# A fused attention and expert kernel: shorter steps for distance and mask tables, paired loads of plain operands, identity products at the start

## The chip, the cores and the metric

The kernel runs on one core of a Trainium2 chip. The metric is the device time of one execution in microseconds (us). The kernel before was run three times: median 1122.09 us, 1121.79 to 1123.15. Line numbers (L892) are those of the kernel before, as its profile gives them.

## The reference

Local attention with a few global columns, then two chains of matrix products. For 4 batches and 8 heads of 64 over 768 positions:

```
scores = q @ k.T / 8
keep   = (column < n_global) | (0 <= row - column < n_local)
dist   = n_local where global and not local, else |row - column|
scores = where(keep, scores - slope[head] * dist, -1e9)
x      = softmax(scores) @ v                  # 3072 tokens of 512
x      = (((x @ w1) * (x @ w2)) @ w3) @ w_out
h      = x @ w_in;   out = (h * cos(h)) @ w_out2
```

`n_global` (8) and `n_local` (96) arrive as 64-bit integers, and the weights as 64-bit floating-point words, which the kernel turns into 32-bit ones itself (the "decoding").

## The kernel before

**Units and chunks.** Attention is cut into 96 units: 128 rows of one pair of heads. A unit's scores are 128 rows by 232 columns for each of its two heads: 128 of its own block, 96 before it and 8 global ones; the first block of a batch has the 128 alone. While `w3 @ w_out` is folded into one matrix in 16 chunks (the loop over `chunks`, c = 0 to 15; a chunk is four 512-wide products, two instructions each at L892), the first 14 units are worked on beside it, unit n = c - 1 in chunk c. A block loop over the remaining units and the products of the experts follows, and then the last part.

**The order in a chunk** is written out by hand and is the order of each engine's queue: the scaled copies of the tables for two heads (`bias_heads`, ScalarE, L514 and L515, in chunks 0 to 3), scores of unit n (TensorE, L575), the load of the plain operands of unit n + 2, values of unit n - 3 (L672), the minimum with the bias (VectorE, L606), decode steps, the exponentials (ScalarE, L617), two of the four products (L892), transposes of unit n - 2 (L645, L647), their copy to SBUF (ScalarE, L655 or L660), the scaling of unit n - 1 by its reciprocal sums (VectorE L627 and L630, ScalarE L636), more decode steps, the other two products.

**Decoding** (`decoder`, a generator called one step at a time). For each weight of 512 KB: a load on SyncE's queue (L325), two passes on ScalarE (L338, L339), then three steps on VectorE: shift (L343), sign (L347), sum (L355). Six buffers hold raw weights, so a load waits for the sum of the sixth weight before it, and whatever stands behind it in SyncE's queue waits too. A chunk needs two decoded weights.

**Before the chunks.** A ScalarE queue loads `v0` (the first values and the two integers) and unit 0's plain operands, and SyncE the first weights. `biases` builds two tables, `dist` (128 by 232) and `d0` (128 by 128), of distances with a very large number where nothing is kept: two casts, then `scalars` (five small steps that turn the integers into floats), four steps ahead of 21 decode steps, and ten more steps, one behind each decode step from the eighth on. The identity for transposes is made on GpSimd. TensorE's first instructions are the scores of unit 0.

**Plain operands.** The first 22 units (`PLAIN`) take queries and keys as they are in 32 bits; a row of 64 partitions holds them, and the input holds them twice, in the lower and the upper 64 partitions. `a_load_plain` puts one unit into the lower half of a tile `hh`, of which there are two, so the load of unit n + 2 waits for the scores of unit n.

Of the kernel before, what the change touches and what calls it, by code (L numbers as in the profile page):

```python
# [8 lines left out]
F32 = mybir.dt.float32  # L9
F32R = mybir.dt.float32r  # L10
I32 = mybir.dt.int32
# [12 lines left out]
LOC, GLB = 96, 8  # L24
# [245 lines left out]
def fused(ctx, tc, a_qk, a_v, a_v0, w3p, wo1p, w1p, w2p, winp, wo2p, out):  # L270
# [164 lines left out]
                )  # L435


    def scalars():
        raw = v0[:, 256:].bitcast(I32).rearrange("p (a b) -> p a b", b=2)
        lo = misc.tile([128, 2], F32, name="nlo")  # L440
        hi = misc.tile([128, 2], F32, name="nhi")
        ng = misc.tile([128, 2], F32, name="nneg")
        nv = misc.tile([128, 2], F32, name="nval")
        nc.vector.tensor_copy(out=lo, in_=raw[:, :, 0])
        nc.vector.tensor_copy(out=hi, in_=raw[:, :, 1])
        nc.vector.tensor_scalar(ng, lo, 0.0, None, ALU.is_lt)
        nc.vector.tensor_tensor(out=hi, in0=hi, in1=ng, op=ALU.add)
        nc.vector.scalar_tensor_tensor(
            out=nv, in0=hi, scalar=4294967296.0, in1=lo, op0=ALU.mult, op1=ALU.add
        )  # L450
        yield nv

    def biases(tp):

        rel = tp.tile([128, 128 + LOC], I32, name="rel")
        col = tp.tile([128, 128], I32, name="col")
        nc.gpsimd.iota(rel[:, 0:128], pattern=[[-1, 128]], base=0, channel_multiplier=1)
        nc.gpsimd.iota(rel[:, 128:], pattern=[[-1, LOC]], base=LOC, channel_multiplier=1)
        nc.gpsimd.iota(col, pattern=[[1, 128]], base=0, channel_multiplier=0)
        dist = tp.tile([128, WIN], F32, name="dist")  # L460
        colf = tp.tile([128, 128], F32, name="colf")
        keep = tp.tile([128, WIN], F32, name="keep")
        lt = rel.bitcast(F32)
        gl = tp.tile([128, 128], F32, name="gl")
        tmp = col.bitcast(F32)
        d0 = tp.tile([128, 128], F32, name="d0")
        nr = 128 + LOC
        nc.vector.tensor_copy(out=dist[:, :nr], in_=rel)
        nc.vector.tensor_copy(out=colf, in_=col)
        yield  # L470
        nv = next(scalars())
        nl, ng = nv[:, 0:1], nv[:, 1:2]
        yield nv
        nc.vector.tensor_scalar(lt[:, :nr], dist[:, :nr], nl, None, ALU.is_lt)
        yield
        nc.vector.scalar_tensor_tensor(
            out=keep[:, :nr], in0=dist[:, :nr], scalar=0.0, in1=lt[:, :nr],
            op0=ALU.is_ge, op1=ALU.mult,
        )
        yield  # L480
        nc.vector.tensor_scalar(gl, colf, ng, None, ALU.is_lt)
        yield
        nc.vector.tensor_copy(out=keep[:, nr:], in_=gl[:, :GLB])
        yield

        nc.vector.tensor_tensor(out=tmp, in0=gl, in1=keep[:, :128], op=ALU.mult)
        yield
        nc.vector.tensor_tensor(out=gl, in0=gl, in1=tmp, op=ALU.subtract)
        yield
        nc.vector.scalar_tensor_tensor(  # L490
            out=tmp, in0=dist[:, :128], scalar=nl, in1=gl, op0=ALU.subtract, op1=ALU.mult
        )
        yield
        nc.vector.tensor_tensor(out=d0, in0=dist[:, :128], in1=tmp, op=ALU.subtract)
        yield
        nc.vector.tensor_tensor(out=tmp, in0=gl, in1=keep[:, :128], op=ALU.add)
        yield

        nc.vector.tensor_scalar(tmp, tmp, -1.0, -FAR, ALU.add, ALU.mult)
        yield  # L500
        nc.vector.tensor_scalar(keep, keep, -1.0, -FAR, ALU.add, ALU.mult)
        yield
        nc.vector.tensor_scalar(dist[:, nr:], colf[:, :GLB], 0.0, nl, ALU.mult, ALU.add)
        yield
        nc.vector.tensor_tensor(out=d0, in0=d0, in1=tmp, op=ALU.add)
        yield
        nc.vector.tensor_tensor(out=dist, in0=dist, in1=keep, op=ALU.add)
        yield d0, dist

    def bias_heads(d0, dist, heads):  # L510

        for h in heads:
            s = -8.0 * 2.0 ** (-8.0 * (h + 1) / H)
            nc.scalar.activation(bias0[:, h, :], d0, ACTF.Copy, scale=s)  # L514
            nc.scalar.activation(bias1[:, h, :], dist, ACTF.Copy, scale=s)  # L515


    def where(n):
        j, r = divmod(n, UPB)
        p, i = divmod(r, TPB)  # L520
        return j, p, i, (TPB * j + i) % (S // 128)
# [8 lines left out]
        nc.sync.dma_start(out=t, in_=a_qk[n])  # L530
        qk_raw[n] = t

    def a_load_plain(n, queue=None):

        if not 0 <= n < PLAIN:
            return
        t = plain[n] = attn.tile([128, QK_W], F32R, tag="hh", name="hh")[0:64].bitcast(F32)
        (queue or nc.sync).dma_start(out=t, in_=a_qk[n, 0:64])

    def a_load_v(n):  # L540
        if not 1 <= n < NU:
# [26 lines left out]
    def a_scores(n):  # L568
        if not 0 <= n < NU:
            return  # L570
        s_ps[n] = p_s.tile([128, 2, WIN], F32, tag="s", name="s_ps")
        if n in plain:
            t, w = plain.pop(n), WIN if where(n)[3] else 128
            for e in range(2):
                nc.tensor.matmul(  # L575
                    s_ps[n][:, e, :w], lhsT=t[:, e * 128:(e + 1) * 128],
                    rhs=t[:, 256 + e * WIN:256 + e * WIN + w], start=True, stop=True,
                )
            return
        t, l = hh.pop(n), kl.pop(n)  # L580
        for e in range(2):
            q = t[:, e * 128:(e + 1) * 128]
            nc.tensor.matmul(  # L583
                s_ps[n][:, e, :], lhsT=q, rhs=t[:, 256 + e * WIN:256 + (e + 1) * WIN],
                start=True, stop=False,
            )
            nc.tensor.matmul(  # L587
                s_ps[n][:, e, :], lhsT=q, rhs=l[:, e * WIN:(e + 1) * WIN],
                start=False, stop=True,
            )  # L590
# [186 lines left out]
    with tc.manual_schedule():  # L777
# [85 lines left out]
        v0 = early.tile([128, 260], F32, name="v0")  # L863
        nc.scalar.dma_start(out=v0, in_=a_v0)
        v_raw[0] = v0[:, :256].rearrange("p (a b) -> p a b", a=2)
        a_load_plain(0, nc.scalar)
        a_scores(0)
        nc.vector.memset(pt_ps, 0.0)
        steps_b = biases(tp)
        next(steps_b)  # L870
        make_identity(nc, ident)
        nv = next(steps_b)
        for _ in range(4):
            next(steps_b)
        dists = None
        for i in range(21):
            decode(1)
            if i == 0:
                a_load_plain(1)
            elif i == 12:  # L880
                a_load_v(1)
            if i > 6:
                dists = dists or next(steps_b)
        W_ps = {}
        for c, (h, k) in enumerate(chunks):
# [18 lines left out]

            a_load(own + 3)
            a_load_v(n - 1 if n > 2 else -1)
            if c < 4:
                bias_heads(*dists, range(2 * c, 2 * c + 2))
            elif c == 4:
                tp.release()  # L910
            if n > 0:
                a_scores(own)
            if n >= 0:
                a_load_plain(own + 2)
            a_values(n - 3)
            a_max(own)
# [509 lines left out]
```

## Time and profile before

| | |
|---|---|
| median of three runs | 1122.09 us |
| profiled execution | 1120.99 us, span 1119.0 us |
| TensorE (PE) | 1100.0 us busy, 98% |
| VectorE (DVE) | 776.6 us, 69% |
| ScalarE (ACT) | 680.4 us, 61% |
| GpSimd (POOL) | 78.8 us, 7% |
| mean granted clock of TensorE | 0.998 of 2.4 GHz |

The span runs from the first to the last instruction. A share is an average over stages: TensorE is full nearly everywhere, the other engines are full in some stretches only. The chain of waits is followed back from the last instruction, so it names at each time the work that the end hung on. `[1.83 <-DVE wo L355]` behind an instruction means that its engine was idle for 1.83 us and that VectorE's L355 ended the idle time. PEld is TensorE's weight load, a q behind an engine its queue. The granted clock of a stretch is given as a share (0.50 is 1.2 GHz).

### The profile page before, as it was taken

Reading aid. Unit: us, or ns where it says so; the run is one execution under the profiler, and the core shown is the slowest. Engines: PE = TensorE matmul, PEld = TensorE weight load, DVE = VectorE, ACT = ScalarE, POOL = GpSimd, SP = SyncE. Lnnn points to the kernel's source line nnn. Section 1 sums busy time; section 2 is a strip of 40 time slices with the busy share of each in tenths; the row PEclk is TensorE's granted clock in tenths of the full one; section 3 lists DMA queues with packets and bytes.
Section 4 is the critical chain, followed back from the end, with each engine's and each line's share of the span. In section 5 each row is a group of like instructions: output and inputs, shape, how many; then the busy total and the mean of one; then the engine's idle time right before and its main releaser. Section 6 shows DMA issues by size and latency. Waiting matters only on the chain.

```text
span 1119.0 us, 17357 instructions
## 1 busy us (share of the span) xinstructions
PE 1100.0 (98%) x6034; PEld 953.0 (85%) x6034; DVE 776.6 (69%) x1661; ACT 680.4 (61%) x1370; POOL 78.8 (7%) x161
## 2 busy tenths in 40 slices
PE   5999999999999999999999999999999999999997
PEld 2456999999999999999999888888888888888886
DVE  8888666767576675778726588884777883877841
ACT  7998766657566676677725466662555561655531
POOL 0000001111111111112200001000000000000000
PEclk9999999999999999999999999999999999999999
DMA  8865545555555556477575545659474458564261
GB/s 305 267 212 177 171 154 187 161 171 165 171 160 180 161 156 194 137 253 237 176 245 189 181 148 214 214 195 377 136 305 179 130 202 346 182 251 170 86 233 60
DMA packets 86480, 219.22 MB, mean 196 GB/s; under 512 B 9328, under 2 KB 25968, under 8 KB 86384
## 3 DMA queue, kind: packets, MB, share of 16 engines
q1 hardware_dynamic: 86016, 217.57, 57.2%
q8 instruction: 50, 0.82, 0.3%
q10 hardware_dynamic: 368, 0.45, 0.1%
q14 instruction: 46, 0.38, 0.1%
HBM read 178.14 MB, written 39.85 MB: 195 GB/s over the span
## 4 chain that ended last, share of the span: by engine, by line
PE 96%; DVE 2%; DMA 1%; issue 0%; ACT 0%; SPq 0%; DVEq 0%
PE mm L432 36%; PE o_ps L432 23%; PE h_ps L432 20%; PE mm L892 4%; PE x_ps L672 4%; PE pt_ps L645 2%; PE s_ps L575 2%; PE pt_ps L647 2%; PE s_ps L587 1%; PE s_ps L583 1%; DMA hh<-in_a_qk 1%; DVE r L1121 0%; DMA v<-in_a_v 0%; DVE w L347 0%; DVE w L355 0%
## 5 line engine op out<-in xcount | busy, mean ns | idle before, releaser
L432 PE MATMUL o_ps<-o,g 128*128 128x512 f32 x960 | 223.3, 389 | 0.0
L432 PEld LDWEIGHTS o_ps<-o,g 128*128 128x128 f32 x960 | 180.0, 188 | 37.6
L432 PE MATMUL mm<-ab,W 128*128 128x384 f32 x768 | 147.0, 342 | 0.0
L432 PE MATMUL mm<-xT,wA 128*128 128x384 f32 x768 | 146.4, 341 | 0.0
L432 PE MATMUL mm<-xT,wB 128*128 128x384 f32 x768 | 146.2, 341 | 0.0
L432 PE MATMUL h_ps<-T,piece 128*128 128x512 f32 x576 | 142.7, 391 | 0.1
L432 PEld LDWEIGHTS mm<-ab,W 128*128 128x128 f32 x768 | 131.5, 188 | 2.7 <-issue 2.4
L432 PEld LDWEIGHTS mm<-xT,wA 128*128 128x128 f32 x768 | 131.1, 188 | 2.1 <-issue 1.8
L432 PEld LDWEIGHTS mm<-xT,wB 128*128 128x128 f32 x768 | 130.9, 188 | 2.1 <-issue 2.1
L432 PEld LDWEIGHTS h_ps<-T,piece 128*128 128x128 f32 x576 | 108.0, 188 | 23.9 <-DVE gr L1235 0.5
L551 ACT CAST hh<-qk 128x720 fp32r<-128x720 f32 x74 | 58.8, 795 | 111.4 <-PE s_ps L587 104.1
L432 PE MATMUL h_ps<-B,piece 128*128 128x512 f32 x432 | 106.5, 390 | 0.0
L638 POOL TENSOR_SCALAR e<-e,st 128x232 f32<-128x232 f32 x148 | 71.8, 496 | 484.3 <-DVE st L630 414.7
L432 PEld LDWEIGHTS h_ps<-B,piece 128*128 128x128 f32 x432 | 81.0, 188 | 17.7 <-DVE vv L1235 0.4
L617 ACT ACTIVATE e<-e,top 128x232 f32<-128x232 f32 (+1 forms) x192 | 89.1, 467 | 1.9 <-DVE top L606 1.8
L606 DVE CUSTOM_DVE_ANT_0 e<-s_ps,bias 128x232 f32<-128x232 f32 (+1 forms) x192 | 65.4, 378 | 31.6 <-PE s_ps L587 27.5
L1127 ACT ACTIVATE r<-r 128x1024 f32<-128x1024 f32 x48 | 51.0, 1062 | 32.4 <-DVE r L1121 32.0
L715 DVE TENSOR_TENSOR a_sb<-mm,a_sb 128x384 f32<-128x384 f32 x64 | 35.6, 556 | 44.4 <-PE mm L432 41.6
L892 PE MATMUL mm<-wo,w 128*128 128x512 f32 x128 | 64.6, 635 | 1.8 <-DVE wo L355 1.8
L1121 DVE SCALAR_TENSOR_TENSOR r<-kt,r 128x1024 f32<-128x1024 int32 x48 | 58.8, 1224 | 1.5
L1140 ACT CAST g<-gr 128x512 fp32r<-128x512 f32 x48 | 29.0, 621 | 42.6 <-PE o_ps L432 42.5
L1145 DVE TENSOR_TENSOR g<-gr,g 128x512 fp32r<-128x512 f32 x48 | 31.7, 687 | 32.4 <-ACT g L1140 32.4
(136 smaller groups left out, 1689.0 us busy)
## 6 DMA issues: line engine op xcount, KB each, us to landing
piece<-a_s SPq DMA_DIRECT2D x84, 512.0 KB, 5.6
o<-o2s SPq DMA_DIRECT2D x80, 512.0 KB, 5.9
qk<-in_a_qk SPq DMA_DIRECT2D x74, 360.0 KB, 3.2
a_s<-ap SPq DMA_DIRECT2D x56, 256.0 KB, 2.4
v<-in_a_v SPq DMA_DIRECT2D x95, 128.0 KB, 3.1
raw<-in_w3p SPq DMA_DIRECT2D x16, 512.0 KB, 5.4
raw<-in_winp SPq DMA_DIRECT2D x16, 512.0 KB, 4.4
raw<-in_wo2p SPq DMA_DIRECT2D x16, 512.0 KB, 4.7
```

What stands on the lines that cost most here:

```text
L432: nc.tensor.matmul(ps, lhsT=l, rhs=r, start=first and i + e == 0, stop=last and i == n - 1 and e == 2, skip_group_check=more,)
L551: nc.scalar.copy(out=hh[n], in_=qk_raw[n])
L606: nc.vector.tensor_tensor_reduce(out=es[n][:, e, :w], in0=sp[:, e, :w], in1=bias[:, 2 * p + e, :], scale=-0.125, scalar=3.0e38, op0=ALU.ad ...
L617: nc.scalar.activation(es[n][:, e, :w], es[n][:, e, :w], ACTF.Exp, bias=top[:, n, e:e + 1], scale=-1.0, accum_out=sts[n][:, 0, e:e + 1],)
L638: nc.gpsimd.tensor_scalar(x, x, st[:, 1, e:e + 1], 1.0, ALU.mult, ALU.mult)
L672: nc.tensor.matmul(x[e * 64:(e + 1) * 64, i * 128:(i + 1) * 128], lhsT=vt[:kk, c, e * 64:(e + 1) * 64], rhs=pt[:kk, e, c, :], start=c == 0 ...
L715: nc.vector.tensor_tensor(out=t, in0=mm_ps.pop("b"), in1=t, op=ALU.mult)
L892: nc.tensor.matmul(W_ps[m], lhsT=wt["w3", c][:, m * 128:(m + 1) * 128], rhs=wt["wo1", k], start=k == 0, stop=k == M1 - 1,)
L1121: nc.vector.scalar_tensor_tensor(out=self.r, in0=self.kt, scalar=-c, in1=self.h if c == C1 else self.r, op0=ALU.mult, op1=ALU.add,)
L1127: nc.scalar.activation(self.r, self.r, ACTF.Sin, scale=0.5)
L1140: nc.scalar.copy(out=t[:, 0, :], in_=src[:, m, :])
L1145: nc.vector.tensor_tensor(out=t[:, 1, :], in0=src[:, m, :], in1=t[:, 0, :].bitcast(F32), op=ALU.subtract,)
```

## The change

`biases` makes the tables in fewer steps. One select on GpSimd puts 2^80 where a column is ahead of its row. Three steps turn the integers into floats. After that come five steps, all between decode steps: distances of `n_local` and more get a multiple of 2^40 added, columns that aren't global 2^120, and `d0` is the smaller of both. `bias_heads` for heads 2 to 7 moves to chunks 3, 6 and 9. A plain tile holds two units, the even one in the lower, the odd one in the upper 64 partitions; one load of 360 KB fetches both (the odd unit from the lower copy in the input and the even one from the upper copy ahead of it). Units 0 and 1 are still loaded apart; the tile of units 2 and 3 is asked for behind the eleventh decode step. Twenty products of the identity with itself, 128 wide, go to TensorE ahead of the scores of unit 0.

```diff
--- before.py
+++ after.py
@@ -435,21 +435,6 @@
                 )
 
 
-    def scalars():
-        raw = v0[:, 256:].bitcast(I32).rearrange("p (a b) -> p a b", b=2)
-        lo = misc.tile([128, 2], F32, name="nlo")
-        hi = misc.tile([128, 2], F32, name="nhi")
-        ng = misc.tile([128, 2], F32, name="nneg")
-        nv = misc.tile([128, 2], F32, name="nval")
-        nc.vector.tensor_copy(out=lo, in_=raw[:, :, 0])
-        nc.vector.tensor_copy(out=hi, in_=raw[:, :, 1])
-        nc.vector.tensor_scalar(ng, lo, 0.0, None, ALU.is_lt)
-        nc.vector.tensor_tensor(out=hi, in0=hi, in1=ng, op=ALU.add)
-        nc.vector.scalar_tensor_tensor(
-            out=nv, in0=hi, scalar=4294967296.0, in1=lo, op0=ALU.mult, op1=ALU.add
-        )
-        yield nv
-
     def biases(tp):
 
         rel = tp.tile([128, 128 + LOC], I32, name="rel")
@@ -459,53 +444,47 @@
         nc.gpsimd.iota(col, pattern=[[1, 128]], base=0, channel_multiplier=0)
         dist = tp.tile([128, WIN], F32, name="dist")
         colf = tp.tile([128, 128], F32, name="colf")
-        keep = tp.tile([128, WIN], F32, name="keep")
-        lt = rel.bitcast(F32)
-        gl = tp.tile([128, 128], F32, name="gl")
-        tmp = col.bitcast(F32)
-        d0 = tp.tile([128, 128], F32, name="d0")
+        past = rel.bitcast(F32)
+        words = misc.tile([128, 2, 2], F32, name="words")
+        nv = misc.tile([128, 2], F32, name="nval")
+        nl, ng = nv[:, 0:1], nv[:, 1:2]
         nr = 128 + LOC
         nc.vector.tensor_copy(out=dist[:, :nr], in_=rel)
         nc.vector.tensor_copy(out=colf, in_=col)
+        nc.gpsimd.affine_select(
+            out=dist[:, :128], in_=dist[:, :128], compare_op=ALU.is_ge, fill=2.0 ** 80,
+            base=0, pattern=[[-1, 128]], channel_multiplier=1,
+        )
         yield
-        nv = next(scalars())
-        nl, ng = nv[:, 0:1], nv[:, 1:2]
+        lo, hi = words[:, :, 0], words[:, :, 1]
+        nc.vector.tensor_copy(
+            out=words.rearrange("p a b -> p (a b)"), in_=v0[:, 256:].bitcast(I32)
+        )
+        nc.vector.scalar_tensor_tensor(
+            out=hi, in0=lo, scalar=0.0, in1=hi, op0=ALU.is_lt, op1=ALU.add
+        )
+        nc.vector.scalar_tensor_tensor(
+            out=nv, in0=hi, scalar=4294967296.0, in1=lo, op0=ALU.mult, op1=ALU.add
+        )
         yield nv
-        nc.vector.tensor_scalar(lt[:, :nr], dist[:, :nr], nl, None, ALU.is_lt)
+        nc.vector.scalar_tensor_tensor(
+            out=past, in0=dist[:, :nr], scalar=nl, in1=dist[:, :nr],
+            op0=ALU.is_ge, op1=ALU.mult,
+        )
         yield
         nc.vector.scalar_tensor_tensor(
-            out=keep[:, :nr], in0=dist[:, :nr], scalar=0.0, in1=lt[:, :nr],
-            op0=ALU.is_ge, op1=ALU.mult,
+            out=dist[:, :nr], in0=past, scalar=2.0 ** 40, in1=dist[:, :nr],
+            op0=ALU.mult, op1=ALU.add,
         )
         yield
-        nc.vector.tensor_scalar(gl, colf, ng, None, ALU.is_lt)
+        nc.vector.tensor_scalar(colf, colf, ng, FAR, ALU.is_ge, ALU.mult)
         yield
-        nc.vector.tensor_copy(out=keep[:, nr:], in_=gl[:, :GLB])
-        yield
-
-        nc.vector.tensor_tensor(out=tmp, in0=gl, in1=keep[:, :128], op=ALU.mult)
-        yield
-        nc.vector.tensor_tensor(out=gl, in0=gl, in1=tmp, op=ALU.subtract)
+        nc.vector.tensor_scalar(dist[:, nr:], colf[:, :GLB], nl, None, ALU.add)
         yield
         nc.vector.scalar_tensor_tensor(
-            out=tmp, in0=dist[:, :128], scalar=nl, in1=gl, op0=ALU.subtract, op1=ALU.mult
-        )
-        yield
-        nc.vector.tensor_tensor(out=d0, in0=dist[:, :128], in1=tmp, op=ALU.subtract)
-        yield
-        nc.vector.tensor_tensor(out=tmp, in0=gl, in1=keep[:, :128], op=ALU.add)
-        yield
-
-        nc.vector.tensor_scalar(tmp, tmp, -1.0, -FAR, ALU.add, ALU.mult)
-        yield
-        nc.vector.tensor_scalar(keep, keep, -1.0, -FAR, ALU.add, ALU.mult)
-        yield
-        nc.vector.tensor_scalar(dist[:, nr:], colf[:, :GLB], 0.0, nl, ALU.mult, ALU.add)
-        yield
-        nc.vector.tensor_tensor(out=d0, in0=d0, in1=tmp, op=ALU.add)
-        yield
-        nc.vector.tensor_tensor(out=dist, in0=dist, in1=keep, op=ALU.add)
-        yield d0, dist
+            out=colf, in0=colf, scalar=nl, in1=dist[:, :128], op0=ALU.add, op1=ALU.min
+        )
+        yield colf, dist
 
     def bias_heads(d0, dist, heads):
 
@@ -530,12 +509,17 @@
         nc.sync.dma_start(out=t, in_=a_qk[n])
         qk_raw[n] = t
 
-    def a_load_plain(n, queue=None):
-
-        if not 0 <= n < PLAIN:
+    def a_load_plain(n, both=True, queue=None):
+
+        if n % 2 and both or not 0 <= n < PLAIN:
             return
-        t = plain[n] = attn.tile([128, QK_W], F32R, tag="hh", name="hh")[0:64].bitcast(F32)
-        (queue or nc.sync).dma_start(out=t, in_=a_qk[n, 0:64])
+        if n % 2 == 0:
+            plain[n // 2] = attn.tile([128, QK_W], F32R, tag="hh", name="hh").bitcast(F32)
+        lo, hi = n % 2 * 64, 128 if both else n % 2 * 64 + 64
+        (queue or nc.sync).dma_start(
+            out=plain[n // 2][lo:hi],
+            in_=a_qk.rearrange("n p c -> (n p) c")[n * 128 + 64:][0:hi - lo],
+        )
 
     def a_load_v(n):
         if not 1 <= n < NU:
@@ -569,8 +553,9 @@
         if not 0 <= n < NU:
             return
         s_ps[n] = p_s.tile([128, 2, WIN], F32, tag="s", name="s_ps")
-        if n in plain:
-            t, w = plain.pop(n), WIN if where(n)[3] else 128
+        if n < PLAIN:
+            t = plain[n // 2][n % 2 * 64:n % 2 * 64 + 64]
+            w = WIN if where(n)[3] else 128
             for e in range(2):
                 nc.tensor.matmul(
                     s_ps[n][:, e, :w], lhsT=t[:, e * 128:(e + 1) * 128],
@@ -863,20 +848,23 @@
         v0 = early.tile([128, 260], F32, name="v0")
         nc.scalar.dma_start(out=v0, in_=a_v0)
         v_raw[0] = v0[:, :256].rearrange("p (a b) -> p a b", a=2)
-        a_load_plain(0, nc.scalar)
-        a_scores(0)
+        a_load_plain(0, False, nc.scalar)
         nc.vector.memset(pt_ps, 0.0)
         steps_b = biases(tp)
         next(steps_b)
         make_identity(nc, ident)
+        warm = p_s.tile([128, 2, WIN], F32, tag="s", name="warm")
+        for _ in range(20):
+            nc.tensor.matmul(warm[:, 0, 0:128], lhsT=ident, rhs=ident, start=True, stop=True)
+        a_scores(0)
         nv = next(steps_b)
-        for _ in range(4):
-            next(steps_b)
         dists = None
         for i in range(21):
             decode(1)
             if i == 0:
-                a_load_plain(1)
+                a_load_plain(1, False)
+            elif i == 10:
+                a_load_plain(2)
             elif i == 12:
                 a_load_v(1)
             if i > 6:
@@ -904,13 +892,13 @@
 
             a_load(own + 3)
             a_load_v(n - 1 if n > 2 else -1)
-            if c < 4:
-                bias_heads(*dists, range(2 * c, 2 * c + 2))
-            elif c == 4:
+            if c % 3 == 0 and c < 12:
+                bias_heads(*dists, range(2 * c // 3, 2 * c // 3 + 2))
+            elif c == 10:
                 tp.release()
             if n > 0:
                 a_scores(own)
-            if n >= 0:
+            if n > 0:
                 a_load_plain(own + 2)
             a_values(n - 3)
             a_max(own)
```

## Rows read from the trace of the kernel before

**Rows 1.** The chain of waits, 0 to 40 us: start us, us, what.
```profile
5.01 0.17 DVE nlo L444
...
5.80 0.35 DVE rel L474
...
6.88 0.43 DVE w L343
...
11.82 0.20 DVE col L486
...
17.36 0.20 DVE d L505
...
21.40 5.63 DMA hh<-in_a_qk
27.16 1.02 PE s_ps L575 x4
...
37.08 1.72 PE mm L892 x4
```

**Rows 2.** Busy time by stretch: us, each engine's busy us, PEclk, DMA share, GB/s.
```profile
20.00:25.00 5.00, 4.68 (x13) 2.11 (x12) 5.00 (x15) 4.36 (x13) 0.00 (x0) 1.00 0.86 277
...
60.00:70.00 10.00, 10.00 (x42) 5.05 (x41) 9.99 (x30) 10.00 (x27) 0.00 (x0) 1.00 0.76 256
```

**Rows 3.** TensorE in order of time: start us, us, instruction [idle before <-releaser].
```profile
7.76 1.22 PE L575 MATMUL s_ps<-hh 64*128 64x128 f32 x4 [7.76 <-DMA hh<-in_a_qk]
...
10.81 9.26 PE L892 MATMUL mm<-wo,w 128*128 128x512 f32 x16 [1.83 <-DVE wo L355]
...
20.98 3.70 PE L892 MATMUL mm<-wo,w 128*128 128x512 f32 x8
...
31.05 0.23 PEld L645 LDWEIGHTS pt_ps<-ident,e 128*128 128x128 f32 x1 [0.15 <-ACT e L636]
```

**Rows 4.** GpSimd, ScalarE and VectorE in order of time, columns as in rows 3.
```profile
1.64 0.33 POOL masks.py:199 TENSOR_SCALAR_AFFINE_SELECT ident<-ident 128x128 f32<-128x128 f32 x1
...
10.31 0.67 ACT L338 ACTIVATE wo<-raw 128x512 f32<-128x512 f32 x1 [0.62 <-DMA raw<-in_wo1p]
...
26.85 0.40 DVE L606 CUSTOM_DVE_ANT_0 e<-s_ps,bias 128x232 f32<-128x232 f32 x1
...
27.18 0.29 ACT L514 ACTIVATE bias<-d 128x128 f32<-128x128 f32 x1
...
28.16 0.47 ACT L617 ACTIVATE e<-e,top 128x232 f32<-128x232 f32 x1
...
30.21 0.68 ACT L636 ACTIVATE e<-e,st 128x128 f32<-128x128 f32 x2
```

**Rows 5.** Busy time in single microseconds, columns as in rows 2.
```profile
11.00:12.00 1.00, 1.00 (x2) 0.48 (x3) 0.96 (x4) 0.55 (x1) 0.00 (x0) 1.00 1.03 410
...
28.00:29.00 1.00, 1.00 (x3) 0.49 (x3) 1.00 (x4) 1.00 (x4) 0.00 (x0) 0.89 1.05 254
29.00:30.00 1.00, 1.00 (x2) 0.33 (x1) 1.00 (x4) 1.00 (x4) 0.00 (x0) 0.50 1.03 273
...
32.00:33.00 1.00, 1.00 (x3) 0.38 (x2) 1.00 (x5) 1.00 (x6) 0.00 (x0) 0.90 1.06 304
```

**Rows 6.** ScalarE's copies L655, L660 and TensorE's L672, columns as in rows 3.
```profile
60.60 0.56 ACT L655 COPY pt<-pt_ps 128x512 f32<-128x512 f32 x1
...
61.48 0.66 PE L672 MATMUL x_ps<-pt,v 128*64 128x128 f32 x8
...
65.77 0.34 ACT L660 COPY pt<-pt_ps 128x256 f32<-128x256 f32 x1
...
66.56 0.44 PE L672 MATMUL x_ps<-pt,v 128*64 128x128 f32 x4
```

**Rows 7.** ScalarE's waits from 40 to 70 us (total, times, longest us).
```profile
ACT e L617 <- DVE top L606: 1.2, 1, 1.2
...
ACT pt L660 <- PE pt_ps L645: 0.2, 1, 0.2
```

## The prediction

> **What bounds the kernel now.** I read the engine totals first: TensorE is busy for 98% of the span, so what the change wins must come from the few stretches in which TensorE isn't fed at full rate. All its parts lie in the first 110 us. So I followed the chain of waits from 0 to 40 us [rows 1]. It runs over VectorE (weight decoding and the tables) from 5 us, then over the load of the third unit's plain operands, `hh`, issued at 21.40 and 5.63 us under way, and then over TensorE. From 37 us on four instructions of L892 take 1.72 us, 0.43 each [rows 1]; the first sixteen took 9.26 us in place of 6.9 [rows 3].
>
> Read like this, TensorE has several things to win: the half-rate start (2.4 us), an earlier first product, the `hh` wait. But another view decides. VectorE is busy in 5.00 of the 5 us from 20 to 25 [rows 2], and the first transpose, that of unit 0, waited at 31.05 for ScalarE's scaling `e` (L636) [rows 3]. TensorE and the chain over VectorE and ScalarE arrive there together, so what TensorE alone wins before 31 us becomes a wait at that transpose. The question is how much earlier this chain gets there.
>
> **The change part by part.**
>
> *Table steps.* VectorE starts at 5.01, when `v0` has landed; five small steps take it to 5.80 [rows 1], so three take 0.5 to 0.6: saved 0.2. The four steps ahead of the decoding, from 5.80 to 6.88 [rows 1], go behind it: 1.08 earlier. Of the ten steps between decode steps (first and last 0.20 each [rows 1], ten make 2.0) five remain. Two are 224 wide, like L474 (0.35 where it waits for its forerunner [rows 1]); between decode steps I price them at 0.3, the other three at 0.15 to 0.25: 1.2, saved 0.8. One wait is new: the fourth weight's first ScalarE pass runs from 10.31 to 10.98 [rows 4], and VectorE now asks for it some 0.2 before that. So VectorE's stream runs 0.2 + 1.08 + 0.8 - 0.2 = 1.9 us earlier from about 18 us on (1.6 to 2.1). The affine select added on GpSimd costs 0.33, the price of the identity's own [rows 4], and the identity is there at about 2.6 us; nothing else waits for it.
>
> *Scaled copies.* A batch for two heads holds ScalarE from 27.18 to 28.16 [rows 4], 0.98 us. Two of four batches leave chunks 1 and 2 for chunks 6 and 9. The exponentials of unit 1 began at 28.16 behind such a batch, though VectorE's minimum that feeds them began at 26.85 [rows 4]. Without it they follow the minimum: 26.85 - 1.9 + 0.55 = 25.5, 2.65 earlier. Between them and unit 0's scaling at 30.21 [rows 4] stand two passes over a weight, as before. So the transpose can start at 31.05 - 2.6 = 28.45. Bounds: 2.0 earlier if a weight lands late, 2.9 if VectorE wins all.
>
> *Paired loads.* The bytes are the same. The tile of units 2 and 3 is asked for in SyncE's queue after the seventh weight, some 13 us earlier, and waits for no buffer: the `hh` wait goes. Late next could be the eighth weight behind it: 360 KB at 410 GB/s, what the stretch from 11 to 12 us moved with its DMA share at 1.03 [rows 5], are 0.9 us. I take 0, since VectorE comes to that weight only behind the last table step (17.36 [rows 1]), even 1.9 sooner some 6 us after the load is asked for; 0.9 would turn the 2.6 into 1.7.
>
> *Identity products.* Twenty, of two instructions each (L575 has x4 for two products), from about 2.6 us on. L575's four took 1.22 us [rows 3], 0.31 each at half rate; a quarter of 0.43 is 0.11 at full rate: they end between 7 and 15. In L892's first sixteen 2.4 us are lost, so half rate lasted some 4.7 us. With as much here, 15 instructions are slow and 25 fast: the end is at 10 to 11 us. Then chunk 0 (8 x 0.43) ends by 14.5, chunk 1 by 18, chunk 2 with its scores (1.02 like those at 27.16 [rows 1], and 3.4) by 22.4, chunk 3's scores and first half (1.0 + 1.7) by 25.1. There TensorE waits until 28.45, 3.3 us: its own gains go into this wait, and the start is worth no more than the 2.6.
>
> *The clock.* TensorE had nothing to do from 24.68 (20.98 + 3.70 [rows 3]) until the load landed at 27.0; the granted clock went to 1.2 GHz at 28.8 and back at 32.2 (0.89, 0.50, 0.90 [rows 5]). Of these 3.4 us at half rate 1.15 lie behind 31.05 and cost 0.6. The new wait is longer. With the same delays (fall 4.1 us after the wait began, return 4.7 to 5.0 after work resumed) the half rate lasts from 29.2 to some 33.3 and costs 2.0: +1.4 against the old 0.6. Bounds: -0.6 without a fall, +1.55.
> The Trainium skill ("TensorE: Matmul & The Clock Gate", Why this matters for your kernels) warns of idle gaps between bursts of matmuls, behind which the clock is at half. The trace agrees for its gap of 2.3 us; by that rule the change's own wait costs the clock once more, and without it the sum would be 2.0 us lower, near the second case below.
>
> *The moved copies, later.* ScalarE is busy in all 10.00 us from 60 to 70 [rows 2]. The copy of unit 5's transposes ends at 61.16, and the products that need it start at 61.48; for unit 6 it is 66.11 and 66.56 [rows 6]: margins of 0.32 and 0.45. A batch of 0.98 in chunk 9 comes in front of the second and pushes TensorE by 0.53. The one in chunk 6 comes in front of the first; by the margin, and less the 0.2 that ScalarE waits for TensorE ahead of an L660 [rows 7], it would push by 0.46. But ScalarE also waits 1.2 us for VectorE there (L617 [rows 7]), which can take it in, unless VectorE is late by ScalarE's lag itself. I take the chunk 9 batch alone, +0.5. Bounds: 0, and 1.96, both in full.
>
> **Sum.** -2.6 + 1.4 + 0.5 = -0.7 us on the profiled execution's 1120.99 (span 1119.0 and 2.0 around it). That execution is 1.1 below the median of the runs, so on the median: 1121.4.
>
> **The rivals.**
> *The clock holds.* If TensorE reaches the transpose later or no fall comes, -2.6 - 0.6 + 0.5 = -2.7: 1119.4; with the batch absorbed too, -3.2: 1118.9. For it: identity products that last longer shorten the wait. Against it: a shorter gap did cost the clock.
> *The scaled copies eat the gain (slower).* Place: ScalarE in chunks 6 to 9; price 1.96 in full; it decides once a batch exceeds the margins of 0.32 and 0.45 and the lag of the first is still there at the second. -2.6 + 1.4 + 1.96 = +0.8, with the start at its lower bound +1.4: 1122.9 to 1123.5. For it: the full row of ScalarE. Against: its idle time of 1.2 us between the two.
> *The identity products don't raise the clock.* They last until 15, chunks 0 and 1 take 9.3 again after the first scores (0.6), chunk 2 and half of chunk 3 another 7.1: 32.0 at the transpose in place of 31.05, without a fall behind it (-0.6) and with the copies (+0.5) +0.85: 1122.9.
> *TensorE keeps all it wins*: 1.3 at the first product, 2.4, 2.3 and the 1.7 that the old fall cost: -7.7, 1114.4. For it stands the chain's name for the wait, the `hh` load; against it the transpose that waits for ScalarE.
>
> **Chances.** Forecast 0.48, clock holds 0.24, copies eat it 0.18, clock not raised 0.06, all kept 0.04. A difference of 0.2% (2.2 us) can be told from none. Faster than 1119.85: three quarters of the second case, the last, and a small tail of the first: 0.25. Slower than 1124.33: tails of the third and fourth: 0.07. Same: 0.68. The forecast's own range is 1120.2 to 1122.8; that of all, without a tenth on each side, 1118.9 to 1123.3.
>
> **What would show it.** Right: VectorE's decode steps about 1.9 us earlier from 18 us on; L892 at 0.43 from its first instruction; no `hh` wait at the third unit's scores; instead TensorE idle for about 3 us ahead of the first L645, released by ScalarE's L636 at about 28.5; half clock for some us behind it; short waits ahead of L672 between 58 and 67 us, released by L655 or L660. Wrong: no wait at the first transpose, or a chunk of the steady stretch reached over 3 us earlier, or later, than before.

## The result, and the profile after

| | before | after |
|---|---|---|
| median of six runs | 1121.64 us | 1127.49 us |
| profiled execution | 1120.99 us, span 1119.0 | 1127.66 us, span 1125.8 |
| TensorE | 1100.0 us busy | 1108.5 us busy |

The ratio is 1.0058 (95% interval 1.0039 to 1.0077): slower, where I forecast 1121.4 us, no difference. Line numbers of the kernel after are 15 lower than those of before from L575 to L672 (L645 is L630, L672 is L657), and 12 lower from L892 on (L892 is L880).

First the stretch that I had forecast. The chain of waits of the kernel after, 0 to 40 us (start, us, what), answers to [rows 1]:

```profile
5.53 0.37 DVE w L343
...
10.41 0.36 DVE rel L470
...
27.96 0.68 ACT e L621 x2
...
32.44 1.91 PE mm L880 x4
```

TensorE in order of time, kernel after, answers to [rows 3]:

```profile
2.52 6.52 PE L858 MATMUL warm<-ident 128*128 128x128 f32 x40 [2.52 <-POOL ident masks.py:199]
...
9.61 3.70 PE L880 MATMUL mm<-wo,w 128*128 128x512 f32 x8
...
23.47 1.98 PE L880 MATMUL mm<-wo,w 128*128 128x512 f32 x4
28.40 0.62 PE L630 MATMUL pt_ps<-ident,e 128*128 128x128 f32 x2 [2.95 <-ACT e L621]
```

The load of `hh` is gone from the chain, L880 runs at full rate from its first instruction (3.70 us for eight), and the first transpose waits for ScalarE's scaling at 28.40, 2.65 earlier than before. TensorE idles 2.95 us ahead of it. Behind this wait the granted clock stayed at 1.00 (2.4 GHz) in this execution; busy time by stretch (columns as in [rows 5]):

```profile
28.00:29.00 1.00, 0.60 (x3) 0.45 (x4) 1.00 (x4) 1.00 (x4) 0.00 (x0) 1.00 0.72 111
29.00:30.00 1.00, 1.00 (x4) 0.43 (x3) 1.00 (x6) 1.00 (x4) 0.00 (x0) 1.00 0.88 293
30.00:31.00 1.00, 1.00 (x5) 0.33 (x3) 1.00 (x4) 1.00 (x4) 0.00 (x0) 1.00 1.01 405
```

Later, ScalarE's copies are late for L657 twice, where the moved scaled copies stand ahead of them; TensorE in order of time, answering to [rows 6]:

```profile
59.52 0.66 PE L657 MATMUL x_ps<-pt,v 128*64 128x128 f32 x8 [0.26 <-ACT pt L640]
...
65.42 0.44 PE L657 MATMUL x_ps<-pt,v 128*64 128x128 f32 x4 [0.76 <-ACT pt L645]
```

So where did 6.8 us of span come from? Three marks in the chains of waits show it: the copy of the last W behind the last product of L892, the first expert product, the last ScalarE copy of the output. Kernel before:

```profile
97.43 0.59 ACT W L900
...
620.14 7.93 PE h_ps L432 x35
...
1112.66 0.39 ACT osb L1180
```

Kernel after:

```profile
96.30 0.59 ACT W L888
...
623.98 4.12 PE h_ps L432 x18
...
1117.11 0.39 ACT osb L1168
```

At 97 us the kernel after leads by 1.13. At the first expert product it is 3.84 behind: 4.97 lost between 97 and 620 us, in the block loop, of which the change touches no line. By the last copy it is 4.45 behind (0.6 more), and at the end of the span 6.8 (2.3 more, behind the last product).

In the block loop TensorE waits for nobody in either kernel (no idle time over 0.1 us from 103 us on). Its products take longer. The same stretch of the chain, before:

```profile
242.88 2.09 PE mm L432 x12
244.96 0.11 PE pt_ps L645
...
247.93 1.47 PE x_ps L672 x24
```

and after:

```profile
242.97 2.12 PE mm L432 x12
245.09 0.11 PE pt_ps L630
...
248.08 1.47 PE x_ps L657 x24
```

Twelve products of 384 columns take 2.12 in place of 2.09; the transposes and the values product are as they were. Part 5 of the page says how general that is; before:

```profile
L432 PE MATMUL mm<-ab,W 128*128 128x384 f32 x768 | 147.0, 342 | 0.0
L432 PE MATMUL mm<-xT,wA 128*128 128x384 f32 x768 | 146.4, 341 | 0.0
L432 PE MATMUL mm<-xT,wB 128*128 128x384 f32 x768 | 146.2, 341 | 0.0
```

and after:

```profile
L432 PE MATMUL mm<-xT,wA 128*128 128x384 f32 x768 | 148.3, 343 | 0.0
L432 PE MATMUL mm<-xT,wB 128*128 128x384 f32 x768 | 148.3, 343 | 0.0
L432 PE MATMUL mm<-ab,W 128*128 128x384 f32 x768 | 148.2, 344 | 0.0
```

The starts of the single products in the traces show two paces: 175 and 172 ns by turns (mean 173.3), or 175, 180, 174, 178 (mean 176.7). I call a group of twelve fast when its last nine distances have a mean below 175 ns: of the 192 groups 145 of before are fast, and none of after.

The end: the last store on SyncE's queue and the queue of instruction fetches (packets, MB, share), before:

```profile
1113.53 0.33 SPq L1183 DMA_DIRECT2D out<-osb  x1
...
q14 instruction: 46, 0.38, 0.1%
```

and after:

```profile
1117.98 0.33 SPq L1171 DMA_DIRECT2D out<-osb  x1
...
q14 instruction: 47, 0.39, 0.1%
```

From that store to the end of the span it is 5.4 us before and 7.8 after, with one packet of instructions more. In the records behind the program's last branch, SyncE of the kernel after waits a second time, from 1121.46 to 1123.92 us, while three more of these 8 KB packets arrive (at 1121.9 to 1122.1). SyncE of the kernel before has no such second wait.

### The profile page after: what moved, and what is told of

Its sections match the earlier page's. It is cut to its first block, busy times and chain, and to the rows that moved or that the text cites. A ratio compares the mean times of both kernels' runs of the same rounds, so it can differ in the third digit from the quotient of the medians.

```text
span 1125.8 us, 17395 instructions
## 1 busy us (share of the span) xinstructions
PE 1108.5 (98%) x6074; PEld 962.7 (86%) x6074; DVE 774.5 (69%) x1650; ACT 680.4 (60%) x1370; POOL 79.3 (7%) x162
## 4 chain that ended last, share of the span: by engine, by line
PE 93%; ACT 3%; DVE 2%; issue 1%; DMA 0%; DVEq 0%; ACTq 0%
PE mm L432 37%; PE o_ps L432 23%; PE h_ps L432 20%; PE x_ps L657 4%; PE mm L880 2%; PE pt_ps L630 2%; PE pt_ps L632 1%; PE s_ps L572 1%; PE s_ps L568 1%; PE s_ps L560 1%; ACT e L602 1%; ACT raw L339 1%; DMA v<-in_a_v 0%; ACT e L621 0%; DVE r L1109 0%
## 5 line engine op out<-in xcount | busy, mean ns | idle before, releaser
L432 PE MATMUL o_ps<-o,g 128*128 128x512 f32 x960 | 223.3, 389 | 0.0
L432 PEld LDWEIGHTS o_ps<-o,g 128*128 128x128 f32 x960 | 180.1, 188 | 37.6
L432 PE MATMUL mm<-xT,wA 128*128 128x384 f32 x768 | 148.3, 343 | 0.0
L432 PE MATMUL mm<-xT,wB 128*128 128x384 f32 x768 | 148.3, 343 | 0.0
L432 PE MATMUL mm<-ab,W 128*128 128x384 f32 x768 | 148.2, 344 | 0.0
L432 PE MATMUL h_ps<-T,piece 128*128 128x512 f32 x576 | 143.1, 392 | 0.1
L432 PEld LDWEIGHTS mm<-ab,W 128*128 128x128 f32 x768 | 132.7, 188 | 2.5 <-issue 2.4
L432 PEld LDWEIGHTS mm<-xT,wA 128*128 128x128 f32 x768 | 132.7, 188 | 2.1 <-issue 1.8
L432 PEld LDWEIGHTS mm<-xT,wB 128*128 128x128 f32 x768 | 132.7, 188 | 2.1 <-issue 2.1
L432 PEld LDWEIGHTS h_ps<-T,piece 128*128 128x128 f32 x576 | 108.0, 188 | 24.3 <-DVE gr L1223 0.5
L432 PE MATMUL h_ps<-B,piece 128*128 128x512 f32 x432 | 106.6, 391 | 0.0
L432 PEld LDWEIGHTS h_ps<-B,piece 128*128 128x128 f32 x432 | 81.1, 188 | 17.8 <-DVE vv L1223 0.4
L880 PE MATMUL mm<-wo,w 128*128 128x512 f32 x128 | 61.2, 605 | 0.9 <-DVE wo L355 0.9
```

What stands on the lines that cost most here:

```text
L432: nc.tensor.matmul(ps, lhsT=l, rhs=r, start=first and i + e == 0, stop=last and i == n - 1 and e == 2, skip_group_check=more,)
L880: nc.tensor.matmul(W_ps[m], lhsT=wt["w3", c][:, m * 128:(m + 1) * 128], rhs=wt["wo1", k], start=k == 0, stop=k == M1 - 1,)
```

## The experiments

What is common to the whole block loop and was changed is where its tiles lie. Before, four small tiles (`nlo`, `nhi`, `nneg`, `nval`) stand ahead of the large ones; after, two. Each takes 32 bytes per partition (the built program has them 32 apart), so every tile behind them on the left side of the on-chip memory lies 64 bytes lower. The weights start at 32 past a multiple of 128 bytes before, at 96 after; the tiles on the right side (xT, ab) don't move. In these products the weights are the stationary operand, the one that PEld loads; xT and ab are the moving operand, the one that the product itself reads. My theory: the place of the weights sets the pace. Rivals: the instruction stream (the identity products), the clock's history, and the attention tiles' place. The ratio is to runs of the kernel before made beside each version, whose medians were 1122.09 to 1122.45; versions made at different times are best compared by it.

| kernel | weights past a multiple of 128 | fast groups of 192 | q14 packets | last store to end | median us | ratio, interval |
|---|---|---|---|---|---|---|
| before | 32 | 145 | 46 | 5.4 | | |
| after | 96 | 0 | 47 | 7.8 | 1127.49 | 1.0058 (1.0039-1.0077) |
| e1_pad | 32 | 134 | 47 | 7.7 | 1122.67 | 1.0004 (0.9995-1.0013) |
| e2_merge | 96 | 0 | 46 | 5.6 | 1128.94 | 1.0050 (1.0037-1.0064) |
| e3_noident | 96 | 0 | 47 | 8.0 | 1127.46 | 1.0047 (1.0033-1.0061) |
| e4_ident | 32 | 144 | 46 | 5.4 | 1122.49 | 1.0001 (0.9992-1.0010) |
| e7_wts | 32 | 105 | 47 | 8.2 | 1124.21 | 1.0019 (1.0009-1.0029) |
| e8_attn | 96 | 0 | 47 | 7.8 | 1128.28 | 1.0050 (1.0032-1.0068) |
| e5_pad1 | 0 | 191 | 47 | 7.8 | 1121.27 | 0.9987 (0.9977-0.9997) |
| e6_pad3 | 64 | 98 | 47 | 7.6 | 1122.23 | 1.0004 (0.9994-1.0014) |
| e9_sync24 | 0 | 191 | 46 | 5.7 | 1119.04 | 0.9963 (0.9950-0.9977) |
| e10_copies | 0 | 191 | 47 | 7.8 | 1123.02 | 1.0010 (1.0001-1.0019) |
| e11_fill | 0 | 191 | 47 | 7.8 | 1121.78 | 0.9995 (0.9986-1.0004) |
| e12_move64 | 0 | 191 | 47 | 8.1 | 1125.08 | 1.0023 (1.0013-1.0033) |
| e13_rel | 64 | 105 | 46 | 5.3 | 1121.91 | 1.0000 (0.9991-1.0009) |
| e14_syncfill | 0 | 191 | 46 | 5.6 | 1119.29 | 0.9976 (0.9966-0.9985) |
| e15_before0 | 0 | 191 | 46 | 5.6 | 1120.90 | 0.9989 (0.9980-0.9998) |

**The place, in both directions.** e1_pad is the kernel after with

```diff
         nv = misc.tile([128, 2], F32, name="nval")
+        misc.tile([128, 2], F32, name="pad0")
+        misc.tile([128, 2], F32, name="pad1")
```

> The kernel after with two unused 32-byte tiles in the pool of small tiles, so that all tiles on the left side of the on-chip memory (weights, decoded words, biases, scores) lie at the addresses of the kernel before, 64 bytes higher than in the kernel after. No instruction changes. Placement theory (the products of the block loop are slower because their operands lie 64 bytes lower): the groups of twelve L432 products return to 2.08-2.10 us, the 5.6 us lost between 97 us and the last product come back, the longer end (7.8 us from the last store's issue in place of 5.4) stays: 1127.5 - 5.6 = 1121.9 us. Instruction-stream theory (the twenty identity products or another count of instructions shift the cadence) and clock-history theory (before fell to half clock once more at 28.8 us, after doesn't): 1127.5, groups at 2.12.

e2_merge is the kernel before with

```diff
-        lo = misc.tile([128, 2], F32, name="nlo")
...
+        three = misc.tile([128, 3, 2], F32, name="three")
+        lo, hi, ng = three[:, 0], three[:, 1], three[:, 2]
```

> The kernel before with the three small tiles nlo, nhi and nneg made slices of one tile, so that all left-side tiles lie 64 bytes lower, as in the kernel after. No instruction changes. Placement theory: groups of L432 at 2.12 us throughout, 1121.6 + 5.6 = about 1127 us, more than any part of the change could cost at the start. Instruction-stream and clock-history theories: 1121.6, groups mixed of 2.08 and 2.12 as before.

Part 5 of e2_merge's page:

```profile
L432 PE MATMUL mm<-xT,wB 128*128 128x384 f32 x768 | 148.4, 343 | 0.0
L432 PE MATMUL mm<-xT,wA 128*128 128x384 f32 x768 | 148.4, 343 | 0.0
L432 PE MATMUL mm<-ab,W 128*128 128x384 f32 x768 | 148.3, 344 | 0.0
```

e1_pad's 1122.67 and e2_merge's 1128.94 stand near where the placement theory put them (1121.9 and 1127), 5 and 7 us from its rivals (1127.5 and 1121.6). Without an instruction changed, 64 bytes lower make the kernel before as slow as the one after, and 64 bytes higher bring the kernel after back: from the first L432 product to the first expert product e1_pad takes 521.9 us, after 526.2, before 521.2. e1_pad keeps the longer end.

**The identity products.** e3_noident takes them out of the kernel after, e4_ident puts them into the kernel before:

```diff
-        warm = p_s.tile([128, 2, WIN], F32, tag="s", name="warm")
-        for _ in range(20):
-            nc.tensor.matmul(warm[:, 0, 0:128], lhsT=ident, rhs=ident, start=True, stop=True)
```

> The kernel after without the twenty identity products (undoes this part alone; placement of after). Placement theory: groups of L432 stay at 2.12; the start loses the early full clock (up to the 2.4 us that L892's first sixteen lost before), most of it in the wait at the first transpose: 1127.5 to 1130. Instruction-stream theory: groups back at 2.08-2.10, 1121.9 to 1123. Clock-history theory: groups back if the clock falls once more after its first rise, at 2.12 if it doesn't.

> The kernel before with the twenty identity products ahead of the first scores and nothing else (placement of before). Placement theory: groups of L432 mixed as before; the products' gain ends in the wait for the third unit's load and the first transpose: 1120 to 1122. Instruction-stream theory: groups at 2.12, about 1127. Clock-history theory: about 1127 if the clock doesn't fall behind its first rise, 1121 if it does.

Neither the pace nor the time moves with them. The clock's history is out as a cause too: the clock of after doesn't fall at 28 us, that of e8_attn (below) falls at 29.1, and both have no fast group.

**Which tiles, which places.** e8_attn has the second line alone, e7_wts both:

```diff
+    wts.tile([128, 16], F32, name="padw", bufs=1)
+    attn.tile([128, 16], F32, name="pada", bufs=1)
```

> The kernel after with 64 unused bytes at the head of the weights' pool and 64 more at the head of the attention pool behind it: the weight tiles (wA, wB, W, piece, g, and B11 to T3 behind them) lie where they do in the kernel before, the attention tiles (hh, e, pt, x, biases) 128 bytes above those of after. Theory that the stationary operands' place sets the cadence: groups of L432 return to the mix of the padded kernel (some 70% at 2.08-2.10 us), last product some 5 us earlier than in after, 1122.5 us. Rival, the attention tiles' place (traffic of VectorE and ScalarE beside the products): all groups at 2.12, 1127.5.

> The kernel after with 64 unused bytes at the head of the attention pool alone: attention tiles lie as before the change, weight tiles as after it. Stationary operands' place: all groups of L432 at 2.12 us, 1127.5. Attention tiles' place: the mix returns, 1122.5.

e5_pad1 and e6_pad3 are e1_pad with one and with three small tiles in place of two.

> The kernel after with one unused 32-byte tile in the pool of small tiles: all left-side tiles 32 bytes higher than in after, 32 lower than in before. If the cadence goes by multiples of 64 bytes (after's weights start at 96 past a multiple of 128, before's at 32), this one, at a multiple of 128, is either as bad as after (1127.5) or better than before; if it went by the bare distance moved, half the loss is left: 1125. I expect 1122 to 1124, with little ground.

> The kernel after with three unused 32-byte tiles: left-side tiles 32 bytes above those of before, 64 past a multiple of 128. If only a start at 96 past a multiple of 128 is bad, 1122.5 or less; if each 32 bytes off before's place cost, 1125 or more. If all groups ran at the fast pace of 173.4 ns a product, the 384-column products would save some 1.8 us on before's mix: 1120.7.

Part 5 of e5_pad1's page:

```profile
L432 PE MATMUL mm<-ab,W 128*128 128x384 f32 x768 | 146.1, 341 | 0.0
L432 PE MATMUL mm<-xT,wA 128*128 128x384 f32 x768 | 146.0, 341 | 0.0
L432 PE MATMUL mm<-xT,wB 128*128 128x384 f32 x768 | 145.9, 340 | 0.0
```

It is the weights, the stationary operands of these products, and not the attention tiles. At a multiple of 128 bytes nearly every group is fast (e5_pad1's 1121.27 is better than my 1122 to 1124), at 96 past one none, at 32 and 64 a part. e1_pad and e7_wts share the weights' place and differ (134 and 105, where I had said some 70%), so in between something else decides too; their attention tiles lie 64 bytes apart, which no run tests at that place.

**The end.** e9_sync24 adds to e5_pad1, in chunks 4 to 14, transfers into a spare DRAM tile:

```diff
+            if 4 <= c < 16:
+                for i in range(2 * c - 8, min(2 * c - 6, 21)):
+                    nc.sync.dma_start(out=spare[i:i + 1], in_=a_v0[0:1, i:i + 1])
```

> The kernel after with one unused 32-byte tile (fast place for the weights, 1121.27 us before) and 21 extra four-byte transfers issued by SyncE in chunks 4 to 14, so that SyncE's program is as long as in the kernel before (after has 24 SyncE instructions fewer, since the plain loads are paired). Theory that the end's length goes by where SyncE's last code lies among the instruction blocks it fetches: from the last store's issue to the end 5.4 us in place of 7.7, so 1121.3 - 2.3 = 1119.0. Rival, the end is longer for another reason (the loads, the stores, the placement): 1121.3, end 7.7.

The last store and q14 of e9_sync24, whose span is 1118.2:

```profile
1112.47 0.33 SPq L1176 DMA_DIRECT2D out<-osb  x1
...
q14 instruction: 46, 0.38, 0.1%
```

Between the profiles this is 2.0 us less than e5_pad1, all behind the last store (5.7 in place of 7.8); between the medians it is 2.2. SyncE's second wait is gone. In all 17 profiles a 47th packet goes with an end of 7.6 to 8.2 us, 46 with 5.3 to 5.7. This version beats both kernels.

**The change's own steps.** e10_copies is e5_pad1 with the scaled copies back:

```diff
-            if c % 3 == 0 and c < 12:
-                bias_heads(*dists, range(2 * c // 3, 2 * c // 3 + 2))
-            elif c == 10:
+            if c < 4:
+                bias_heads(*dists, range(2 * c, 2 * c + 2))
+            elif c == 4:
```

> The kernel after with one unused 32-byte tile, and with the scaled copies put back in chunks 0 to 3 (undoes this part alone). My step: the copies moved to chunks 6 and 9 cost 0.5 of the 2.65 us that their move wins at the first transpose. Then here the first transpose starts at about 29.3 in place of 28.3, TensorE's waits for ScalarE between 58 and 67 us (0.8 to 1.4 us in all) go, and the first L432 product starts between 98.0 and 99.0 (97.4 to 98.5 in the kernels with moved copies): 1121.3 to 1122.0. If the moved copies cost all that they win, no difference at 97 us; if they cost nothing, 99 or later.

TensorE's waits up to 100 us in e10_copies (total, times, longest us; the added line of padding makes L630 L631 here):

```profile
PE pt_ps L631 <- ACT e L622: 4.7, 1, 4.7
PE warm L859 <- POOL ident masks.py:199: 2.5, 1, 2.5
```

and in e5_pad1:

```profile
PE pt_ps L631 <- ACT e L622: 2.8, 1, 2.8
...
PE x_ps L658 <- ACT pt L646: 0.8, 1, 0.8
PE x_ps L658 <- ACT pt L641: 0.3, 1, 0.3
```

The waits for the copies at 58 to 67 us go, as I said; but the first transpose is 1.66 later (29.94 against 28.28; I had said 1.0), behind the longer wait the clock is at 0.50 for 10.2 us, and the first L432 product starts at 101.43, where I had 98.0 to 99.0. The kernel is slower than e5_pad1, by 1.8 us between the medians, by 2.6 between the ratios. Moving the copies pays, and by more than my step said.

e11_fill and e14_syncfill put this in front of the first transposes of e5_pad1 and e9_sync24:

```diff
+            if n == 2:
+                for _ in range(10):
+                    nc.tensor.matmul(
+                        pt_ps[:, 0, 0, :], lhsT=ident, rhs=ident, start=True, stop=True
+                    )
```

> The kernel after with one unused 32-byte tile and ten more identity products right ahead of the first transposes, where TensorE waits 2.9 us for ScalarE; they write to a part of the transposes' bank that the transposes overwrite. If the idle wait is what lets the granted clock fall at 28 to 29 us in some executions (it fell in three of seven profiles of kernels with this wait, and the first L432 starts 0.9 us later in those), no profile or run falls any more: 0.9 us less in such executions, 1120.4 on the median. If the clock goes by something else: 1121.3.

> The kernel with the 21 extra SyncE transfers (1119.04 us) and the ten identity products ahead of the first transposes. If the wait's fall of the clock is what separates its executions (1117.8 to 1120.0), all come to about 1118.2. If what the ten products win at 97 us (1.1) is lost later to a load, as in the profile of the kernel with them alone (0.5 us of wait for o2s, last product 0.3 earlier), 1118.8.

The clock fell in neither profile, and the first L432 product starts at 97.34 and 97.23 (98.45 and 98.53 without the fill). Two profiles are few, since without a fill three of nine keep the clock too. The medians don't show it (1121.78 and 1119.29, where I had 1120.4 and 1118.2): e11_fill's profile gives 0.8 back behind the first expert product, 0.5 of it in a wait for a load of `o` at 920 us, but e14_syncfill's doesn't, with its last product 1.55 earlier than e9_sync24's and a span of 1116.5; other executions of it took up to 2.3 us more. That stays open.

**Stationary place alone?** e12_move64 shifts the expert products' moving operands, e13_rel shifts weights and right-side tiles together:

```diff
+                    x2cA.tile([128, 16], F32, name="padx")
...
-    edge.tile([128, 8], F32, name="edge")
+    edge.tile([128, 24], F32, name="edge")
```

> The kernel after with one unused 32-byte tile (weights at a multiple of 128 bytes) and 64 unused bytes ahead of the moving operands of the first expert products (B11 to T3), which then start at 64 past a multiple of 128, as in the kernel with three unused tiles, whose h_ps products took 389 ns in place of 391. If the moving operand's place makes this difference, the 1008 products take 1.5 us less: 1119.8. If it is the stationary piece's place, 1121.3 and 391 ns.

> The kernel with the 21 extra SyncE transfers (1119.04 us), with three unused small tiles (weights at 64 past a multiple of 128 bytes) and 64 bytes more at the right edge, so that the moving operands xT and ab start at a multiple of 128 in place of 64 past one: the weights stand to them as in that kernel, both moved by 64. If the pace goes by how stationary and moving operands stand to each other, all groups of L432 stay at 2.08 us, and h_ps (both operands at 64, as with three unused tiles alone) takes 389 ns: 1119.0 - 1.5 = 1117.5. If it goes by the stationary place alone, half of the groups are at 2.12 as with three unused tiles, +1.6 - 1.5: 1119.1.

For the 384-column products the stationary place decides: e13_rel has 105 fast groups and takes 522.7 us from the first L432 product to the first expert product; e6_pad3, with the weights at the same place and the moving operands 64 bytes higher, has 98 and takes 522.8 (e5_pad1 520.1). This comparison was made at 64 past a multiple alone.

For the 512-column products of the experts I have no rule: e6_pad3 has h_ps at 389 ns, e12_move64 at 392, e13_rel at 390 to 391. My expectations failed there, and with them the times: e12_move64 took 1125.08 in place of 1119.8 or 1121.3. Part 5 of e5_pad1's page:

```profile
L432 PE MATMUL o_ps<-o,g 128*128 128x512 f32 x960 | 223.3, 389 | 0.0
L432 PE MATMUL h_ps<-T,piece 128*128 128x512 f32 x576 | 142.8, 391 | 0.1
```

and of e12_move64's:

```profile
L432 PE MATMUL o_ps<-o,g 128*128 128x512 f32 x960 | 224.7, 391 | 0.0
L432 PE MATMUL h_ps<-T,piece 128*128 128x512 f32 x576 | 143.3, 392 | 0.1
```

The edit moves the six tiles B11 to T3 and nothing else; every stationary operand is where it was, and the part from the first expert product to the last takes 495.9 us in place of 493.0. So for these products the moving operand's place counts as well; why `o_ps`, whose own operands don't move, slows with them is open. Most of the rest of e12_move64's loss is half clock for 6.8 us at the start (first L432 product at 99.64, 98.45 in e5_pad1). e13_rel took 1121.91 in place of 1117.5 or 1119.1: half clock for 6.8 us (first L432 product 1.55 later than e9_sync24's) and 2.55 us in the block loop, where I had 1.6.

e15_before0 gives the kernel before the good place (`nlo` and `nhi` slices of one tile):

> The kernel before with two of its small tiles made one, so that the weights start at a multiple of 128 bytes; SyncE's program unchanged. By the runs so far: all groups of L432 at 2.08 us, 1.8 us less than before, 1120.3. The kernel after at this place and with this length of SyncE's program took 1119.04, so that the change by itself would be worth about 1.2 us (my forecast said 0.7). If the place at a multiple of 128 helps only the changed kernel: 1122.1.

The good place helps the kernel before too. With weights at the same place and an end of the same kind, the change is worth 1120.90 - 1119.04 = 1.9 us between medians taken at different times, 2.9 us by the ratios (0.9963 against 0.9989), and 1.3 between the spans of the two profiles (1119.5 and 1118.2).

## Why the prediction was wrong

The steps at the start came out near their numbers.
- *Table steps*: VectorE's minimum of unit 1 begins at 25.11 against 26.85 [rows 4], 1.74 earlier (forecast 1.9).
- *Scaled copies and the first transpose*: unit 1's exponentials at 25.90 (forecast 25.5), the transpose at 28.40 (28.45), after a wait of 2.95 (3.3).
- *Paired loads*: the `hh` wait went, and TensorE waits for no other load in its place.
- *Identity products*: they end at 9.0 (forecast 10 to 11) and, as forecast, win nothing by themselves: without them e3_noident took 1127.46.
- *The clock*: I took one case where there are two. Of nine profiles with this wait (2.65 to 3.03 us) and no fill, six show the fall, between 28.2 and 29.5 us; those of after, e1_pad and e6_pad3 don't. Where the half rate lasted 3.4 us the first L432 product came 0.9 to 1.4 us later than e1_pad's 97.48 (98.39 in e7_wts, 98.45 in e5_pad1, 98.88 in e8_attn), where it lasted 6.8 us 2.2 and 2.6 later (99.64 in e12_move64, 100.08 in e13_rel); I had 2.0 for some 4.1 us. The Trainium skill ("TensorE: Matmul & The Clock Gate", Why this matters for your kernels) warns of idle gaps between bursts of matmuls. Here that holds as a risk: a gap of 2.65 to 3.03 us was followed by half clock in six profiles and not in three.
- *The moved copies*: 0.26 + 0.76 = 1.0 in chunks 6 and 9, where I took 0.5 for the second alone. The lead fell from 2.3 (the scores at 36.51 us in the chain of after, 38.80 before) to 1.13 at 97 us.
- *A wait that the sum didn't have*: at 32.00 us L657 waits 0.62 for ScalarE's copy L645; the kernel before has no wait there.

Together, -1.13 us at 97 us against -0.7 in the sum. That these are so near is luck in part: in this execution the clock held, for which my second case says -2.7, and the 0.62 and the 0.5 more for the moved copies took most of the difference. The sentence that failed is "All its parts lie in the first 110 us", and with it the sum, which took everything behind as unchanged. The change also removes two small tiles and 24 of SyncE's instructions. The first moved all weights to the one place of four at which no group is fast (4.97 + 0.6 us; e1_pad wins back 4.3 and 0.6 of this, and has 11 fast groups fewer than before). The second made the end 2.4 us longer, with a 47th packet and a second wait of SyncE; that the added transfers of e9_sync24 undo it shows the cause, while its working, one more fetch of code, is read from the packets. -1.13 + 5.6 + 2.35 = 6.8, the difference of the spans. None of my rivals had it; the two that ended on the slower side put their price ahead of 70 us and reached 1123.5 at most.

## What to carry to other kernels

An edit that adds or drops a small tile moves every tile behind it: compare the mean duration of untouched products (here 341 to 342 against 343 to 344 ns over 2304 of them) before explaining a difference by what was edited, and test it with an unused tile. Where TensorE is busy for 98% of the span, 2% of a product's pace can outweigh the stalls of the start (here 5.6 us against the 1.13 won by 97 us), so try the four places that differ by 32 bytes before judging a change, and judge it with tiles at equal places.

## What the hardware showed

- Products of 384 columns ran at a mean of 173.1 ns from start to start with the stationary operand at a multiple of 128 bytes (e5_pad1), at 176.7 with it at 96 past one (after), and mixed at 32 and 64. Why 96 past a multiple is the bad place, and what chooses at 32 and 64, isn't settled.
- With products of 512 columns the moving operands' place counted too: 64 bytes under B11 to T3 cost 2.9 us over the experts (e12_move64 against e5_pad1).
- The end of a program cost 2.1 us more with 21 transfers fewer in one engine's program (7.8 us in e5_pad1, 5.7 in e9_sync24), with 47 packets on the instruction queue in place of 46.
- The same instructions behind an idle gap of 2.9 us ahead of the first transposes ran on at a granted clock of 1.00 in e1_pad, and behind one of 2.8 us fell to 0.50 in e5_pad1, which has 32 bytes of padding less; e5_pad1:

```profile
29.00:30.00 1.00, 1.00 (x3) 0.32 (x2) 1.00 (x5) 1.00 (x4) 0.00 (x0) 0.66 1.02 363
30.00:31.00 1.00, 1.00 (x3) 0.20 (x1) 1.00 (x4) 1.00 (x6) 0.00 (x0) 0.50 1.10 344
```
